# Decode attention with a gated feed-forward: weights in long runs with permuted d and f, loads in another order, down projection by rows

## The chip, the cores and the metric

One core of a Trainium2 chip runs the whole program. The metric is the device time of one execution in microseconds (us). It is about 1.8 to 2 us more than the span that a profile shows, from the first instruction to the last. Repeated executions of the kernel before lie within 0.3 to 0.7 us of each other on one chip, so differences of one microsecond can be read against it. The experiments ran on other chips in three series, each beside the kernel before, whose median was 1316.80, 1316.98 and 1316.93 us there, so medians of different series can be compared.

## The reference, cut to what matters

```python
# B=4 tokens, D=512, H=32 heads of Dh=128, caches of Sk=8192 rows, F=1792, all bf16
x  = A_x
q  = layernorm(x) @ wq                                   # wq 512 x 4096
s  = einsum("bhqd,bhkd->bhqk", q, k_cache) * Dh ** -0.5
o  = einsum("bhqk,bhkd->bhqd", softmax(s), v_cache)
h  = x + o.reshape(B, 1, H * Dh) @ wo                    # wo 4096 x 512
hn = layernorm(h)
h2 = h + (sigmoid(hn @ w_gate) * (hn @ w_up)) @ w_down   # 512 x 1792, 1792 x 512
```

The two caches are 537 MB, the five weights 14 MB. Every byte is read once.

## The kernel before

The caches come in 256 loads of 2 MB, one for each of k and v of each token and head, into a ring of eight slots. One list gives the order of all loads, and the sync engine (SP) issues them in that order, each when its slot is free. v runs ten loads behind k. The v tiles are called v0 to v127 below.

```python
items = [("wq", 0)]
for t in range(NT + LAG):            # NT = 128, LAG = 10
    if t < NT:
        items.append(("k", t))
    if t == NT + 3:
        items.append(("wo", 0))      # ahead of v121
    if t == NT + LAG - 1:
        items.append(("wg", 0))      # ahead of v127
    if t >= LAG:
        items.append(("v", t - LAG))
items += [("wu", 0), ("wd", 0)]      # behind v127
...
# the output weights go where the transposed k was, so their load waits for the last score
op.deps = [sc_of[NT - 1]] if it[0] == "wo" else [consumed[p] for p in prev_of[it]]
```

The weights are loaded so that the contraction index is on the 128 partitions in blocks: `wq`, gate and up with `"(c p) f -> p c f"`, down with `"(t p) f -> p t f"`, the output weights with `"(h p) f -> p h f"`. A matmul has two operands. In the profiles each matmul has two records, a weight load (PEld, 11846 in the kernel before) and the matmul itself (PE, 11846 too), and the weight loads run beside the matmuls (gate and up: 3.06 us of PEld and 3.15 us of PE, both from 1303.79 us). The operand of the weight load is called stationary here, the other one moving. The results are written to PSUM, the accumulators. In the tail of the kernel all weights are the stationary operand, in blocks of 128 adjacent columns, and the activations (4 columns, one a token) are the moving one:

```python
def wo_mms(e, heads, b0, b1, first=False):          # 160 matmuls in all
    ... e.matmul(bH[...], wo_v[:, h, 128 * c:128 * (c + 1)], OT[...], ...)

def pe_gu(e, wv, bk):                               # gate, then up: 56 matmuls each
    for t in range(NFT):                            # NFT = 14
        for c in range(NDC):                        # NDC = 4
            e.matmul(bk[:, B * t:B * t + B], wv[:, c, 128 * t:128 * (t + 1)],
                     hnT[:, B * c:B * c + B], start=(c == 0), stop=(c == NDC - 1))

def pe_down(e):                                     # 56 matmuls, result is h2 transposed
    for c in range(NDC):
        for t in range(NFT):
            e.matmul(bX[:, B * c:B * c + B], wd_v[:, t, 128 * c:128 * (c + 1)],
                     hh_sb[:, B * t:B * t + B], start=(t == 0), stop=(t == NFT - 1))
# then: add h (VectorE), four fp32 transposes, one copy of 4 x 512, output DMA
```

Of the kernel before, what the change touches and what calls it, by code (L numbers as in the profile page):

```python
# [6 lines left out]
FP32 = mybir.dt.float32  # L7
U32 = mybir.dt.uint32
ALU = mybir.AluOpType
ACT = mybir.ActivationFunctionType  # L10
# [3 lines left out]
LAG = 10  # L14
# [58 lines left out]
def bass_sequential_preLN__mha_block_cached__glu_gated_glu__decode_kernel(  # L73
# [12 lines left out]
    B, _sq, D = A_x.shape  # L86
    _, H, S, DH = A_k_cache.shape
    F = B_w_gate.shape[1]
    assert DH == 128 and H == 32 and D == 512 and F % 128 == 0 and B <= 4
    assert S == 8192  # L90
    NDC = D // 128
    NFT = F // 128
    NT = B * H
    NG = NT // GH
    R = S // 128
    TW = R * 128
# [4 lines left out]
    P = prog.add  # L101

    with ExitStack() as es:
        def SB(name, shape, dt):
            return es.enter_context(nc.sbuf_tensor(name, shape, dt))
# [8 lines left out]
        ident = SB("ident", [128, 128], BF16)  # L114
        identf = SB("identf", [128, 128], FP32)
# [5 lines left out]
        xpad = SB("xpad", [128, D], BF16)  # L121
        x_bf = SB("x_bf", [128, D], BF16)
# [16 lines left out]
        hnT = SB("hnT", [128, NDC * B], BF16)  # L139
        sg_sb = SB("sg_sb", [128, NFT * B], FP32)  # L140
        hh_sb = SB("hh_sb", [128, NFT * B], BF16)
        oT_f = SB("oT_f", [128, NDC * B], FP32)
        o_sb = SB("o_sb", [B, D], BF16)

        PS = es.enter_context(nc.psum_tensor("PS", [128, 4096], FP32))
# [2 lines left out]
        bX, bH = bank[6], bank[7]  # L148
# [8 lines left out]
        def ringv(slot):  # L157
            return ring[:, slot, :]


        items = [("wq", 0)]
        for t in range(NT + LAG):
            if t < NT:
                items.append(("k", t))
            if t == NT + 3:
                items.append(("wo", 0))
            if t == NT + LAG - 1:
                items.append(("wg", 0))
            if t >= LAG:
                items.append(("v", t - LAG))  # L170
        items += [("wu", 0), ("wd", 0)]
        slot_of, prev_of, dma_of = {}, {}, {}
        owner = [None] * (NS - 1) + [("qr", 0)]
        uses = [0] * NS
# [21 lines left out]
        def kv_src(t, cache):  # L196
            return cache[t // H, t % H, :, :].rearrange("(p r) d -> p (r d)", p=128)

        dma_x = P("sp", lambda e: e.dma_start(x_bf[0:B, :], A_x.rearrange("b s d -> (b s) d")).then_inc(s_x, 16),
                  sem=s_x, val=16)  # L200

        def load(it):
            kind, t = it
            slot = slot_of.get(it)
            if kind == "wo":
                return [(lambda e: e.dma_start(wo_v, A_wo.rearrange("(h p) f -> p h f", p=128)).then_inc(s_wo, 16),
                         s_wo, 16)]
            if kind == "v" and t == NT - 1:
                ops = []
                for i in range(4):  # L210
                    def f(e, i=i):
                        c0 = i * (TW // 4)
                        return e.dma_start(ringv(slot)[:, c0:c0 + TW // 4],  # L213
                                           kv_src(t, A_v_cache)[:, c0:c0 + TW // 4]).then_inc(s_piece[i], 16)
                    ops.append((f, s_piece[i], 16))
                return ops
            uses[slot] += 1
            sem, val = s_slot[slot], 16 * uses[slot]
            if kind == "k":
                dst, src = ringv(slot), kv_src(t, A_k_cache)  # L220
            elif kind == "v":
                dst, src = ringv(slot), kv_src(t, A_v_cache)
            elif kind == "wq":
                dst, src = wq_v, A_wq.rearrange("(c p) f -> p c f", p=128)
            elif kind == "wg":
                dst, src = wg_v, B_w_gate.rearrange("(c p) f -> p c f", p=128)
            elif kind == "wu":
                dst, src = wu_v, B_w_up.rearrange("(c p) f -> p c f", p=128)
            else:
                dst, src = wd_v, B_w_down.rearrange("(t p) f -> p t f", p=128)  # L230
            return [(lambda e: e.dma_start(dst, src).then_inc(sem, 16), sem, val)]  # L231


# [37 lines left out]
        def pe_xT(e):  # L271
            mm = None
            for c in range(NDC):
                mm = e.matmul(bX[:, B * c:B * c + B], x_bf[0:B, 128 * c:128 * (c + 1)], ident[0:B, 0:B],
                              start=True, stop=True)
            return mm
        p_xT = P("pe", pe_xT, [dma_x, c_ident])

        def pe_xnT(e):
            mm = None  # L280
            for c in range(NDC):
                mm = e.matmul(bH[:, B * c:B * c + B], xpad[:, 128 * c:128 * (c + 1)], ident[:, 0:B],
                              start=True, stop=True)
            return mm
        p_xnT = P("pe", pe_xnT, [d_x, c_ident])
# [20 lines left out]
        for half in range(2):  # L306
            for a in range(4):
                def f(e, half=half, a=a):
                    dst = bass.AP(ring, QR0 + half * 2048 + 32 * a,
                                  [[NS * TW, 128], [256, 8], [128, 2], [1, 32]])  # L310
                    src = bS[half][:, :].rearrange("p (g w e) -> p g e w", g=8, e=2)
                    if half == 0:
                        return e.activation(dst, src, ACT.Copy)
                    return e.tensor_copy(dst, src)  # L314
# [71 lines left out]
        def pe_pv(t, r0=0, r1=R, last=True):  # L386
            it = ("v", t)
            g, hh = t // GH, t % GH
            slot = slot_of[it]
            ob = bO[(g + (1 if t == NT - 1 else 0)) % 2]  # L390

            def f(e):
                mm = None
                for r in range(r0, r1):
                    c0 = (r % 16) * 32 + (r // 16) * 8 + hh
                    mm = e.matmul(ob[:, hh:hh + 1], ringv(slot)[:, r * 128:(r + 1) * 128],  # L396
                                  PT_sb[:, g % 2, c0:c0 + 1], start=(r == 0), stop=(r == R - 1))
                return mm
            deps = [ptc_of[g]]
            if t == NT - 1:  # L400
                deps += [dma_of[it][r0 // 16]]
            else:
                deps += dma_of[it]
            if hh == 0:
                deps.append(oev_of.get(g - 2))
            if t == NT - 1:
                deps.append(oev_of.get(g - 1))
            op = P("pe", f, deps)
            if last:
                pv_of[t] = op  # L410
                consumed[it] = op
# [105 lines left out]
        def wo_mms(e, heads, b0, b1, first=False):  # L517
            mm = None
            for h in heads:
                for c in range(NDC):  # L520
                    mm = e.matmul(bH[:, c * B + b0:c * B + b1], wo_v[:, h, 128 * c:128 * (c + 1)],
                                  OT[:, b0 * H + h:(b1 - 1) * H + h + 1:H],
                                  start=(first and h == heads[0] and c == 0),
                                  stop=(h == H - 1 and c == NDC - 1), skip_group_check=True)
            return mm
# [4 lines left out]
        o_a = oev(gl, 0, GH - 1)  # L530
        P("pe", lambda e: wo_mms(e, range(H - GH, H - 1), B - 1, B), [o_a])
        P("act", lambda e: e.activation(lnst[0:B, 9:10], lnst[0:B, 3:4], ACT.Sqrt), [exp_of[gl]])
        for i in range(4):
            pe_pv(NT - 1, 16 * i, 16 * i + 16, last=(i == 3))
        o_b = oev(gl, GH - 1, GH)
        p_attn = P("pe", lambda e: wo_mms(e, range(H - 1, H), B - 1, B), [o_b])

# [21 lines left out]
                                                  mean_b(20), ALU.mult), [d_rs, d_hc])  # L559
        P("act", lambda e: e.activation(lnst[0:B, 10:11], tst[0:B, 12:13], ACT.Sigmoid), [a_sq])  # L560

        def pe_gu(e, wv, bk):
            mm = None
            for t in range(NFT):
                for c in range(NDC):
                    mm = e.matmul(bk[:, B * t:B * t + B], wv[:, c, 128 * t:128 * (t + 1)],
                                  hnT[:, B * c:B * c + B], start=(c == 0), stop=(c == NDC - 1))
            return mm
        p_g = P("pe", lambda e: pe_gu(e, wg_v, bS[0]), [d_hn, dma_of[("wg", 0)][0]])
# [1 line left out]
        a_sig = P("act", lambda e: e.activation(sg_sb[:, :], bS[0][:, 0:NFT * B], ACT.Sigmoid), [p_g])  # L571
        d_hh = P("dve", lambda e: e.tensor_tensor(hh_sb[:, :], sg_sb[:, :], bS[1][:, 0:NFT * B], ALU.mult), [a_sig, p_u])

        def pe_down(e):
            mm = None
            for c in range(NDC):
                for t in range(NFT):
                    mm = e.matmul(bX[:, B * c:B * c + B], wd_v[:, t, 128 * c:128 * (c + 1)],  # L578
                                  hh_sb[:, B * t:B * t + B], start=(t == 0), stop=(t == NFT - 1))
            return mm  # L580
        p_d = P("pe", pe_down, [d_hh, dma_of[("wd", 0)][0], d_st])
        d_o = P("dve", lambda e: e.tensor_tensor(oT_f[:, :], h2[:, 0, :], bX[:, 0:NB], ALU.add), [p_d])

        def pe_oT(e):
            mm = None
            for c in range(NDC):
                mm = e.transpose(bP[0][0:B, 128 * c:128 * (c + 1)], oT_f[:, B * c:B * c + B], identf[:, :])  # L587
            return mm
        p_oT = P("pe", pe_oT, [d_o, ptc_of[gl], ptc_of[gl - 1]])
        d_out = P("dve", lambda e: e.tensor_copy(o_sb[:, :], bP[0][0:B, 0:D]), [p_oT])  # L590
        consumed[("wg", 0)] = consumed[("wu", 0)] = consumed[("wd", 0)] = p_d

        def sp_out(e):
            e.dma_start(out.rearrange("b s d -> (b s) d"), o_sb[:, :]).then_inc(s_out, 16)
            return e.wait_ge(s_out, 16)
        P("sp", sp_out, [d_out])

        for it in items:
            for op in dma_of[it]:
# [51 lines left out]
```

## Time and profile before

| | before |
|---|---|
| time, median of 4 | 1316.81 us (1316.69 to 1316.97) |
| span of the profiled run | 1314.9 us |
| DMA queue, share of 16 engines | 99.1% |
| landing of the last weights (down) | 1309.44 us |
| from that landing to the end | 5.5 us |

The page of the kernel before says what bounds it. In the second part each digit is the busy share of one fortieth of the span in tenths:

```profile
PE   2453443433343353343344344344334434334425
DMA  9999999999999999999999999999999999999997
GB/s 391 428 427 426 428 426 428 426 426 427 427 427 427 428 427 425 427 427 428 426 427 428 427 426 428 426 428 427 426 427 427 426 428 425 429 426 428 371 381 292
...
q1 hardware_dynamic: 44816, 550.79, 99.1%
```

The DMA engines are busy from end to end at about 427 GB/s and TensorE (PE) is 40% busy. Only in the last three slices does the rate fall. The windows view (start:end, length, busy time and count of PE, PEld, VectorE (DVE), ScalarE (ACT) and GpSimd (POOL), PE clock, DMA share, GB/s) shows a hole there. The clock of 1.00 in these lines is a missing record:

```profile
1200.00:1203.00 3.00, 0.00 (x0) 0.00 (x0) 3.00 (x4) 0.00 (x0) 0.00 (x0) 1.00 0.97 410
1230.00:1233.00 3.00, 0.00 (x0) 0.00 (x0) 3.00 (x4) 0.00 (x0) 0.00 (x0) 1.00 0.71 295
1233.00:1236.00 3.00, 2.29 (x33) 0.90 (x34) 0.99 (x2) 0.00 (x0) 0.00 (x0) 1.00 0.57 246
...
1251.00:1254.00 3.00, 0.00 (x0) 0.00 (x0) 0.00 (x0) 0.00 (x0) 0.00 (x0) 1.00 0.54 190
```

The tail of the kernel before, from the timeline (start us, duration us, engine, line, operation, count, and in brackets the idle time before and what ended it; PEld lines, the weight loads that run beside the matmuls, are left out):

```profile
1290.56 1.87 PE L396 MATMUL PS<-PT_sb,ring 128*128 128x1 bf16 x64 [4.17 <-DMA ring<-in_A_v_cache_dram]
...
1292.29 4.30 PE L521 MATMUL PS<-OT,kT 128*128 128x4 bf16 x156
...
1298.66 1.42 PE L396 MATMUL PS<-PT_sb,ring 128*128 128x1 bf16 x48 [2.07 <-issue]
...
1303.79 3.15 PE L566 MATMUL PS<-hnT,ring 128*128 128x4 bf16 x112 [1.34 <-DVE hnT L557]
...
1309.57 1.64 PE L578 MATMUL PS<-hh_sb,ring 128*128 128x4 bf16 x56 [2.64 <-DMA ring<-in_B_w_down_dram]
1311.24 0.17 DVE L582 TENSOR_TENSOR oT_f<-h,PS 128x16 f32<-128x16 f32 x1 [3.99 <-PE PS L578]
...
1311.47 1.01 PE L587 MATMUL PS<-identf,oT_f 128*4 128x128 f32 x4 [0.27 <-DVE oT_f L582]
1312.52 0.68 DVE L590 CAST o_sb<-PS 4x512 bf16<-4x512 f32 x1 [1.10 <-PE PS L587]
```

Gate and up are 112 matmuls in 3.15 us, 28 ns each. TensorE is then idle for 2.64 us until the down weights land: here the DMA decides, and only the work behind that landing counts.

One more reading is needed. The trace records sixteen completion increments for each load. I read them as one for each of the core's 16 DMA engines; the records do not name the engine. For some loads of the kernel before, worked out from these records:

```
load                  last of 16 at   the sixteen came earlier than that by (us)
an early k            73.54           1.7 ... 1.4, 1.4, 1.4, 1.1, 1.1, 0.7, 0.0, 0.0
a v half way          608.38          8.2 8.1 7.9 7.8 7.5 7.4 7.3 5.1 | 0.4 0.3 0.3 0.3 0.3 0.2 0.1 0.0
v120                  1248.99         17.8 17.6 17.4 17.3 16.9 16.4 16.1 11.8 | 2.3 2.0 1.8 0.6 0.6 0.5 0.3 0.0
output weights        1260.00         10.2 to 9.9 (eight) | 2.2 to 0.0 (eight)
down weights          1309.44         4.7 to 3.7 (eight) | 1.4 to 0.0 (eight)
```

Eight engines come to run ahead of the other eight, by up to 17.8 us just ahead of the output weights; behind them the lead is about 4 us. A load has landed only when the last of the sixteen has come: the matmuls on v120, whose last came at 1248.99 us, begin at 1249.13. So the late eight set the landings.

### The profile page before, as it was taken

The numbers are of one execution on the slowest core, as the hardware profiler recorded it, in microseconds if no ns is written. First come the engines' busy times: TensorE is split into PE (matmuls) and PEld (weight loads), VectorE is DVE, ScalarE is ACT, GpSimd is POOL, SyncE is SP. The second block draws the span as 40 slices with busy tenths as digits, with TensorE's granted clock in tenths as the row PEclk, the third lists the DMA queues.
The fourth block names the chain that finished last, engine by engine and source line by source line (L and its number), as shares of the span: only waits on it lengthen the run. The fifth ranks groups of instructions, "written<-read, shape, count | busy, mean of one in ns | idle before, by whom it ended". The sixth has DMA issues, their size and how long they took to land.

```text
span 1314.9 us, 24889 instructions
## 1 busy us (share of the span) xinstructions
PE 522.6 (40%) x11846; PEld 327.6 (25%) x11846; DVE 629.1 (48%) x640; ACT 38.9 (3%) x86; POOL 9.7 (1%) x17
## 2 busy tenths in 40 slices
PE   2453443433343353343344344344334434334425
PEld 1122222222232232222222222222222223222324
DVE  6975445445444544544544454554544444454300
ACT  3000000000000000000000000000000000000000
POOL 2000000000000000000000000000000000000000
DMA  9999999999999999999999999999999999999997
GB/s 391 428 427 426 428 426 428 426 426 427 427 427 427 428 427 425 427 427 428 426 427 428 427 426 428 426 428 427 426 427 427 426 428 425 429 426 428 371 381 292
DMA packets 44917, 552.37 MB, mean 420 GB/s; under 512 B 4232, under 2 KB 10128, under 8 KB 11664
## 3 DMA queue, kind: packets, MB, share of 16 engines
q1 hardware_dynamic: 44816, 550.79, 99.1%
q8 instruction: 92, 1.51, 0.5%
q14 instruction: 9, 0.07, 0.0%
HBM read 550.77 MB, written 0.00 MB: 419 GB/s over the span
## 4 chain that ended last, share of the span: by engine, by line
DMA 82%; DVE 12%; issue 3%; SPq 2%; PE 1%
DMA ring<-in_A_k_cache_dram 77%; DVE kT L356 11%; DMA ring<-in_A_v_cache_dram 2%; DMA ring<-in_B_w_down_dram 2%; SPq L213 1%; DMA ring<-in_A_wq_dram 1%; DVE Lq L339 0%; SPq L231 0%; PE PS L396 0%; PE PS L373 0%; PE PS L297 0%; DVE ring L314 0%; PE PS L324 0%; PE PS L578 0%; PE PS L587 0%
## 5 line engine op out<-in xcount | busy, mean ns | idle before, releaser
L356 DVE STREAM_TRANSPOSE kT<-ring 128x1024 uint32<-128x1024 uint32 x512 | 592.3, 1213 | 596.0 <-DMA ring<-in_A_k_cache_dram 596.0
L373 PE MATMUL PS<-kT,Lq 128*32 128x512 bf16 x2048 | 242.8, 623 | 663.5 <-DVE kT L356 663.5
L396 PEld LDWEIGHTS PS<-PT_sb,ring 128*128 128x128 bf16 x8192 | 230.1, 104 | 116.1 <-issue 75.5
L396 PE MATMUL PS<-PT_sb,ring 128*128 128x1 bf16 x8192 | 239.3, 165 | 39.7 <-DMA ring<-in_A_v_cache_dram 36.5
L373 PEld LDWEIGHTS PS<-kT,Lq 128*32 128x32 bf16 x2048 | 56.8, 126 | 751.3 <-DVE kT L356 679.8
L435 ACT ACTIVATE negm<-PS 128x1 f32<-128x1 f32 x16 | 2.7, 171 | 1166.9 <-PE PS L431 1166.9
L446 PE MATMUL PS<-LS,onesf 128*128 128x8 f32 x32 | 9.5, 372 | 65.2 <-DVE LS L442 65.2
L468 DVE TENSOR_TENSOR OT<-PS,rinv 128x8 bf16<-128x8 f32 (+2 forms) x17 | 2.0, 115 | 53.4 <-PE PS L396 53.4
L446 PEld LDWEIGHTS PS<-LS,onesf 128*128 128x128 f32 x32 | 8.0, 311 | 66.8 <-DVE LS L442 66.8
L457 PE MATMUL PS<-Sel,E_sb 128*32 128x32 bf16 x1024 | 11.4, 193 | 2.5 <-issue 1.4
L414 DVE TENSOR_REDUCE mx<-PS 128x1 f32<-128x512 f32 x16 | 10.5, 657 | 2.0 <-PE PS L373 2.0
L431 PEld LDWEIGHTS PS<-onesf,rowx 1*128 1x128 f32 x32 | 8.0, 307 | 12.6 <-issue 12.6
L437 ACT ACTIVATE E_sb<-PS,negm 128x512 bf16<-128x512 f32 x16 | 11.0, 687 | 0.7 <-ACT negm L435 0.2
L463 ACT ACTIVATE PT_sb<-PS 128x512 bf16<-128x512 f32 x16 | 9.6, 597 | 27.0 <-PE PS L457 27.0
L457 PEld LDWEIGHTS PS<-Sel,E_sb 128*32 128x32 bf16 x1024 | 9.6, 103 | 2.8 <-issue 1.5
L431 PE MATMUL PS<-onesf,rowx 1*128 1x1 f32 x32 | 9.3, 358 | 0.0
L249 POOL MEMSET Lq<- 128x8208 f32 x1 | 6.9, 6937 | 0.0
L339 DVE CAST Lq<-PS 32x128 bf16<-32x128 f32 x8 | 5.7, 712 | 2.2 <-PE PS L324 2.0
L267 DVE TENSOR_SCALAR xpad<-x_bf,lnst 4x512 bf16<-4x512 bf16 x1 | 6.0, 5993 | 0.0
L420 PE MATMUL PS<-identf,mx 128*1 128x128 f32 x16 | 5.9, 371 | 0.0
L314 DVE CAST ring<-PS 128x512 bf16<-128x512 f32 x4 | 2.5, 684 | 7.2 <-PE PS L297 7.2
L338 ACT ACTIVATE Lq<-PS 32x128 bf16<-32x128 f32 x8 | 5.7, 715 | 4.3 <-PE PS L324 4.1
(69 smaller groups left out, 67.5 us busy)
## 6 DMA issues: line engine op xcount, KB each, us to landing
ring<-in_A_k_cache_dram SPq DMA_DIRECT2D x128, 2048.0 KB, 34.7
ring<-in_A_v_cache_dram SPq DMA_DIRECT2D x127, 2048.0 KB, 35.9
ring<-in_A_wq_dram SPq DMA_DIRECT2D x1, 4096.0 KB, 12.5
kT<-in_A_wo_dram SPq DMA_DIRECT2D x1, 4096.0 KB, 24.3
ring<-in_A_v_cache_dram SPq DMA_DIRECT2D x4, 512.0 KB, 28.0
ring<-in_B_w_gate_dram SPq DMA_DIRECT2D x1, 1792.0 KB, 37.8
ring<-in_B_w_up_dram SPq DMA_DIRECT2D x1, 1792.0 KB, 23.4
ring<-in_B_w_down_dram SPq DMA_DIRECT2D x1, 1792.0 KB, 23.7
```

What stands on the lines that cost most here:

```text
L213: return e.dma_start(ringv(slot)[:, c0:c0 + TW // 4], kv_src(t, A_v_cache)[:, c0:c0 + TW // 4]).then_inc(s_piece[i], 16)
L249: zlq = pool(lambda e: e.memset(Lq[:, :].bitcast(FP32), 0.0))
L267: d_x = P("dve", lambda e: e.tensor_scalar(xpad[0:B, :], x_bf[0:B, :], st[0:B, 0:1], st[0:B, 4:5], op0=ALU.subtract, op1=ALU.mult), [d_r, zx])
L356: return e.transpose(kT[:, buf, i * q:(i + 1) * q].bitcast(U32), ringv(src)[:, i * q:(i + 1) * q].bitcast(U32))
L373: mm = e.matmul(bS[g % 2][32 * j:32 * (j + 1), :], Lq[:, l0:l0 + 32], rhs, start=(hh == 0 and v == 0), stop=(hh == GH - 1 and v == 3), til ...
L396: mm = e.matmul(ob[:, hh:hh + 1], ringv(slot)[:, r * 128:(r + 1) * 128], PT_sb[:, g % 2, c0:c0 + 1], start=(r == 0), stop=(r == R - 1))
L414: mx_of[g] = P("dve", lambda e: e.tensor_reduce(mx[:, :], bS[g % 2][:, :], AX.X, ALU.max), [sc_of[g * GH + GH - 1], p1_of.get(g - 1)])
L431: p2_of[g] = P("pe", lambda e: e.matmul(bX[:, 0:1], rowx[0:1, :], onesf[0:1, 0:1], start=True, stop=True), [d2b_of[g], c_ones])
L437: exp_of[g] = P("act", lambda e: e.activation(E_sb[:, :], bS[g % 2][:, :], ACT.Exp, bias=negm[:, 0:1], scale=SCALE, accum_out=sig[:, 0:1]) ...
L446: L_of[g] = P("pe", lambda e: e.matmul(bX[:, 0:GH], onesf[:, :], LS[:, :], start=True, stop=True), [LS_of[g], a1_of[g], c_ones])
L457: mm = e.matmul(bP[g % 2][32 * a:32 * (a + 1), 32 * rr:32 * rr + 32], E_sb[:, 32 * rr:32 * rr + 32], Sel[:, a, :], start=True, stop=True, ...
L463: ptc_of[g] = P("act", lambda e: e.activation(PT_sb[:, g % 2, :], bP[g % 2][:, :], ACT.Copy), [pt_of[g]] + last_pv)
```

## The change

The intent: long contiguous runs in DRAM for `wq`, gate, up and down, by renumbering d as 4p+c and f as 14p+t; the output weights just ahead of v126 instead of v121, so that the other loads do not queue behind them; all feed-forward weights behind v127; v127 in two pieces instead of four; the input x on the ACT queue; and the down projection by rows, with the activations stationary and the weights moving, so that the result needs no transposes. h is put into the same accumulators ahead of time by small fp32 matmuls against an identity.

```diff
-            if t == NT + 3:
+            if t == NT + LAG - 2:
                 items.append(("wo", 0))
-            if t == NT + LAG - 1:
-                items.append(("wg", 0))
             if t >= LAG:
                 items.append(("v", t - LAG))
-        items += [("wu", 0), ("wd", 0)]
+        items += [("wg", 0), ("wu", 0), ("wd", 0)]
@@ ... x on the ACT queue, v127 in two pieces, down weights in two parts (10 and 4 of t)
-                dst, src = wq_v, A_wq.rearrange("(c p) f -> p c f", p=128)
+                dst, src = wq_v, A_wq.rearrange("(p c) f -> p c f", p=128)
@@ ... gate and up alike; down:
-                dst, src = wd_v, B_w_down.rearrange("(t p) f -> p t f", p=128)
+                          ... B_w_down.rearrange("(p t) f -> p t f", p=128)[:, t0:t1, :]
@@ ... output projection, gate and up: the stationary operand is now strided
-    wo_v[:, h, 128 * c:128 * (c + 1)]
+    wo_v[:, h, c:D:NDC]                    # step 4 elements, 8 bytes
-    wv[:, c, 128 * t:128 * (t + 1)]
+    wv[:, c, t:F:NFT]                      # step 14 elements, 28 bytes
@@ ... h by rows, ahead of gate
+        def pe_h(e):
+            for s_ in range(2):
+                for c in range(NDC):
+                    mm = e.matmul(bP[s_][0:B, c:HD:NDC], h2[:, 0, B * c:B * c + B],
+                                  identf[:, 64 * s_:64 * s_ + 64], start=(c == 0), stop=False, ...)
@@ ... down by rows; the addition, the transposes and the copy of 4 x 512 go
+        for i, (t0, t1) in enumerate(WD_PARTS):
+            for s_ in range(2):
+                    for t in range(t0, t1):
+                        mm = e.matmul(bP[s_][0:B, 0:HD], hh_sb[:, B * t:B * t + B],
+                                      wd_v[:, t, HD * s_:HD * s_ + HD], start=False, ...)
+        o0 = P("act", ... activation(o_sb[:, 0:HD], bP[0][0:B, 0:HD], ACT.Copy) ...)
+        o1 = P("dve", ... tensor_copy(o_sb[:, HD:D], bP[1][0:B, 0:HD]) ...)
```

More of the change, by code (lines that the diff above doesn't have):

```diff
@@ L141, in bass_sequential_preLN__mha_block_cached__glu_gated_glu__decode_kernel @@
         hh_sb = SB("hh_sb", [128, NFT * B], BF16)
-        oT_f = SB("oT_f", [128, NDC * B], FP32)
         o_sb = SB("o_sb", [B, D], BF16)
@@ L158, in ringv @@
             return ring[:, slot, :]
+        WD_PARTS = [(0, 10), (10, NFT)]
         items = [("wq", 0)]
@@ L197, in kv_src @@
             return cache[t // H, t % H, :, :].rearrange("(p r) d -> p (r d)", p=128)
-        dma_x = P("sp", lambda e: e.dma_start(x_bf[0:B, :], A_x.rearrange("b s d -> (b s) d")).then_inc(s_x, 16),
+        dma_x = P("act", lambda e: e.dma_start(x_bf[0:B, :], A_x.rearrange("b s d -> (b s) d")).then_inc(s_x, 16),
                   sem=s_x, val=16)
@@ L209, in load, with f @@
                 ops = []
-                for i in range(4):
+                for i in range(2):
                     def f(e, i=i):
-                        c0 = i * (TW // 4)
-                        return e.dma_start(ringv(slot)[:, c0:c0 + TW // 4],
-                                           kv_src(t, A_v_cache)[:, c0:c0 + TW // 4]).then_inc(s_piece[i], 16)
+                        c0 = i * (TW // 2)
+                        return e.dma_start(ringv(slot)[:, c0:c0 + TW // 2],
+                                           kv_src(t, A_v_cache)[:, c0:c0 + TW // 2]).then_inc(s_piece[i], 16)
                     ops.append((f, s_piece[i], 16))
+                return ops
+            if kind == "wd":
+                ops = []
+                for i, (t0, t1) in enumerate(WD_PARTS):
+                    def f(e, t0=t0, t1=t1, i=i):
+                        return e.dma_start(wd_v[:, t0:t1, :],
+                                           B_w_down.rearrange("(p t) f -> p t f", p=128)[:, t0:t1, :]
+                                           ).then_inc(s_piece[2 + i], 16)
+                    ops.append((f, s_piece[2 + i], 16))
                 return ops
@@ L223, in load @@
             elif kind == "wq":
-                dst, src = wq_v, A_wq.rearrange("(c p) f -> p c f", p=128)
+                dst, src = wq_v, A_wq.rearrange("(p c) f -> p c f", p=128)
             elif kind == "wg":
-                dst, src = wg_v, B_w_gate.rearrange("(c p) f -> p c f", p=128)
-            elif kind == "wu":
-                dst, src = wu_v, B_w_up.rearrange("(c p) f -> p c f", p=128)
+                dst, src = wg_v, B_w_gate.rearrange("(p c) f -> p c f", p=128)
             else:
-                dst, src = wd_v, B_w_down.rearrange("(t p) f -> p t f", p=128)
+                dst, src = wu_v, B_w_up.rearrange("(p c) f -> p c f", p=128)
             return [(lambda e: e.dma_start(dst, src).then_inc(sem, 16), sem, val)]
@@ L273, in pe_xT @@
             for c in range(NDC):
-                mm = e.matmul(bX[:, B * c:B * c + B], x_bf[0:B, 128 * c:128 * (c + 1)], ident[0:B, 0:B],
+                mm = e.matmul(bX[:, B * c:B * c + B], x_bf[0:B, c:D:NDC], ident[0:B, 0:B],
                               start=True, stop=True)
@@ L281, in pe_xnT @@
             for c in range(NDC):
-                mm = e.matmul(bH[:, B * c:B * c + B], xpad[:, 128 * c:128 * (c + 1)], ident[:, 0:B],
+                mm = e.matmul(bH[:, B * c:B * c + B], xpad[:, c:D:NDC], ident[:, 0:B],
                               start=True, stop=True)
@@ L400, in pe_pv @@
             if t == NT - 1:
-                deps += [dma_of[it][r0 // 16]]
+                deps += [dma_of[it][r0 // 32]]
             else:
@@ L520, in wo_mms @@
                 for c in range(NDC):
-                    mm = e.matmul(bH[:, c * B + b0:c * B + b1], wo_v[:, h, 128 * c:128 * (c + 1)],
+                    mm = e.matmul(bH[:, c * B + b0:c * B + b1], wo_v[:, h, c:D:NDC],
                                   OT[:, b0 * H + h:(b1 - 1) * H + h + 1:H],
@@ L532, in bass_sequential_preLN__mha_block_cached__glu_gated_glu__decode_kernel @@
         P("act", lambda e: e.activation(lnst[0:B, 9:10], lnst[0:B, 3:4], ACT.Sqrt), [exp_of[gl]])
-        for i in range(4):
-            pe_pv(NT - 1, 16 * i, 16 * i + 16, last=(i == 3))
+        for i in range(2):
+            pe_pv(NT - 1, 32 * i, 32 * i + 32, last=(i == 1))
         o_b = oev(gl, GH - 1, GH)
@@ L560, in bass_sequential_preLN__mha_block_cached__glu_gated_glu__decode_kernel @@
         P("act", lambda e: e.activation(lnst[0:B, 10:11], tst[0:B, 12:13], ACT.Sigmoid), [a_sq])
+        HD = D // 2
+        def pe_h(e):
+            mm = None
+            for s_ in range(2):
+                for c in range(NDC):
+                    mm = e.matmul(bP[s_][0:B, c:HD:NDC], h2[:, 0, B * c:B * c + B], identf[:, 64 * s_:64 * s_ + 64],
+                                  start=(c == 0), stop=False, skip_group_check=True)
+            return mm
+        P("pe", pe_h, [d_h, c_identf, ptc_of[gl], ptc_of[gl - 1]])
         def pe_gu(e, wv, bk):
@@ L565, in pe_gu @@
                 for c in range(NDC):
-                    mm = e.matmul(bk[:, B * t:B * t + B], wv[:, c, 128 * t:128 * (t + 1)],
+                    mm = e.matmul(bk[:, B * t:B * t + B], wv[:, c, t:F:NFT],
                                   hnT[:, B * c:B * c + B], start=(c == 0), stop=(c == NDC - 1))
@@ L572, in bass_sequential_preLN__mha_block_cached__glu_gated_glu__decode_kernel, with pe_down @@
         d_hh = P("dve", lambda e: e.tensor_tensor(hh_sb[:, :], sg_sb[:, :], bS[1][:, 0:NFT * B], ALU.mult), [a_sig, p_u])
-        def pe_down(e):
-            mm = None
-            for c in range(NDC):
-                for t in range(NFT):
-                    mm = e.matmul(bX[:, B * c:B * c + B], wd_v[:, t, 128 * c:128 * (c + 1)],
-                                  hh_sb[:, B * t:B * t + B], start=(t == 0), stop=(t == NFT - 1))
-            return mm
-        p_d = P("pe", pe_down, [d_hh, dma_of[("wd", 0)][0], d_st])
-        d_o = P("dve", lambda e: e.tensor_tensor(oT_f[:, :], h2[:, 0, :], bX[:, 0:NB], ALU.add), [p_d])
-        def pe_oT(e):
-            mm = None
-            for c in range(NDC):
-                mm = e.transpose(bP[0][0:B, 128 * c:128 * (c + 1)], oT_f[:, B * c:B * c + B], identf[:, :])
-            return mm
-        p_oT = P("pe", pe_oT, [d_o, ptc_of[gl], ptc_of[gl - 1]])
-        d_out = P("dve", lambda e: e.tensor_copy(o_sb[:, :], bP[0][0:B, 0:D]), [p_oT])
-        consumed[("wg", 0)] = consumed[("wu", 0)] = consumed[("wd", 0)] = p_d
+        p_d = []
+        for i, (t0, t1) in enumerate(WD_PARTS):
+            for s_ in range(2):
+                def pe_down(e, t0=t0, t1=t1, s_=s_):
+                    mm = None
+                    for t in range(t0, t1):
+                        mm = e.matmul(bP[s_][0:B, 0:HD], hh_sb[:, B * t:B * t + B], wd_v[:, t, HD * s_:HD * s_ + HD],
+                                      start=False, stop=(t == NFT - 1), skip_group_check=True)
+                    return mm
+                p_d.append(P("pe", pe_down, [d_hh, dma_of[("wd", 0)][i]]))
+        o0 = P("act", lambda e: e.activation(o_sb[:, 0:HD], bP[0][0:B, 0:HD], ACT.Copy), [p_d[2]])
+        o1 = P("dve", lambda e: e.tensor_copy(o_sb[:, HD:D], bP[1][0:B, 0:HD]), [p_d[3]])
+        consumed[("wg", 0)] = consumed[("wu", 0)] = consumed[("wd", 0)] = p_d[3]
         def sp_out(e):
@@ L595, in sp_out @@
             return e.wait_ge(s_out, 16)
-        P("sp", sp_out, [d_out])
+        P("sp", sp_out, [o0, o1])
         for it in items:
```

## The prediction

> **What bounds the kernel now.** DMA: the slices show the DMA engines 9/10 busy throughout, 427 GB/s in the middle; the DMA queue took 99.1% of 16 engines' span; the chain of waits is 82% DMA. From 2.3 to 1309.4 us some engine always transfers; then a tail of 5.5 us (timeline): down projection 1.64, addition 0.17, transposes 1.0, copy 0.68, output DMA about 1.7.
>
> The windows show the DMA share falling to 0.57 at 1233-1236 us and 0.54 at 1251-1254: the sync queue stood 21.4 us waiting for the last score before the output-weight load, then 18.3 us issuing the next value load behind that load's 4096 small packets. The lost share sums to about 7.8 us, which I do not count as gain. The sixteen completion increments of each load show eight engines up to 17 us ahead of the other eight by then. Landings are set by the late eight, which never starve: v120 lands at 1248.99, the output weights 11.0 us later, then a value load each 4.9 us. The hole eats only the early engines' lead; moving the load moves the hole.
>
> **What changes, on the late engines.**
> - Start: the x load leaves the sync queue; weights start 0.4 us earlier.
> - Packet records: 16 KB takes 615 ns, 4 KB about 168, 3.5 KB 143, 1 KB 41 to 50. [...] The last value goes from 5.36 us to an estimated 4.95, gate and up from 4.32 and 4.62 to about 4.3 each, down from 4.63 to about 4.4: together about 1 us. The output weights keep 1 KB rows.
> - The last landing comes at about 1308.0.
> - Tail: after the last part only 8 matmuls of 256 columns (estimate 0.9 us), two half copies side by side (0.4), output DMA (1.7): 3.2 us if nothing before is late. Eight fp32 matmuls (about 1.3 us) put h into PSUM under the layer norm.
>
> **The risk is TensorE before the end.** Feed-forward weights now follow the last value, so from v126's landing (about 1290.1) TensorE must do 64 value matmuls, 156 of the output projection (4.3 us), the last value, layer norm, gate, up, then 20 down matmuls. At today's weight-load rate (27 ns each) these end just as the last weights land. But the permutation makes weight loads strided: 8 bytes for output weights, 28 for gate and up. [...] Unslowed, I get a span of 1311.3; gate and up at half speed (3.1 us each), 1313.5; output weights slow too, about 1318.
>
> **Prediction.** The time is 2 us over the span: 1314.6 us, range 1312.4 to 1318.5. Chances: over 2% faster 0.01, within 2% 0.98, over 2% slower 0.01.
>
> **Shown by:** landings (last weights about 1308, each value 4.9 us on the late half); the DMA-share hole still there, about 30 us later; spacing of weight loads in gate and up; the wait ahead of the last 8 down matmuls (DMA or TensorE's own work); tail from last landing to end 3 to 6 us.
>
> **What would make it wrong:** strided weight loads at four times the time (slower than before); late engines gaining when the early ones keep streaming (2 to 8 us faster); fp32 matmuls delaying gate.

Two sentences, one on small packets and one on strided weight loads, are cut from the recorded text where it is marked: they did not come from the traces of this case. The sum itself came to this: last landing at 1308.0 us and a tail of 3.2 us, a span of 1311.3 with nothing slowed; 1313.5 if gate and up take twice their 3.1 us together; the point, 1314.6 less the 2 us, is a span of 1312.6, between the two. That a strided weight load might go at half speed was my supposition; no trace had shown what a step costs. The estimates for the loads follow from packet times: 256 packets of 8 KB, 309 ns each in the trace of the kernel before (the query weights, median), on 16 engines are 4.94 us for the last value. Averaged, the packets of that trace took 616 ns at 16 KB, 170 at 4 KB, 143 at 3.5 KB and 46 to 50 at 1 KB. Two estimates do not say from what they are: 0.9 us for the last 8 matmuls (the kernel after: 109 ns each, 0.87 us, at the full clock, and 213 ns each at the half clock) and 1.3 us for the fp32 matmuls (1.87 us there).

## The result, and the profile after

| | before | after |
|---|---|---|
| time, median of 4 | 1316.81 us | 1319.51 us (1318.65 to 1320.16) |
| ratio | | 1.002, 95% interval 1.0003 to 1.0037 |
| span of the profiled run | 1314.9 us | 1316.9 us |
| landing of the query weights | 13.71 us | 12.90 us |
| landing of the last weights | 1309.44 us | 1308.13 us |
| from there to the end | 5.5 us | 8.8 us |

Ratios are the mean time of one kernel's fast runs over that of the other's of the same rounds, so they are not quite the ratios of the medians. Their intervals reach about 0.15% (2 us) to each side; for differences of a few microseconds I also give the single runs. In a second series of five rounds the changed kernel took 1320.09 us against 1316.93, ratio 1.0025 (1.0011 to 1.0039). By the rule of 2% this is "same", but it is slower, and it was predicted faster.

The slices of the page after, with a line for the clock that TensorE was granted:

```profile
PEclk7555555555555555555555555555555555555555
GB/s 400 429 426 428 427 427 427 427 428 425 426 428 426 428 427 426 426 427 428 427 428 426 427 426 428 428 427 428 425 427 427 427 426 427 427 427 427 427 319 266
```

The rate now holds until the last two slices. The windows of the kernel after show that the hole has moved, and the last three of them what the clock does at the end (0.50 in this view is half of TensorE's full clock):

```profile
1230.00:1233.00 3.00, 0.00 (x0) 0.00 (x0) 3.00 (x4) 0.00 (x0) 0.00 (x0) 0.50 1.02 426
...
1269.00:1272.00 3.00, 0.90 (x34) 0.81 (x31) 0.00 (x0) 0.00 (x0) 0.00 (x0) 0.50 0.54 224
1272.00:1275.00 3.00, 1.87 (x64) 1.79 (x64) 0.00 (x0) 0.00 (x0) 0.00 (x0) 0.50 0.53 188
...
1308.00:1311.00 3.00, 2.62 (x34) 2.20 (x34) 0.21 (x1) 0.00 (x0) 0.00 (x0) 0.50 0.00 0
1311.00:1314.00 3.00, 3.00 (x21) 2.00 (x20) 0.00 (x0) 0.00 (x0) 0.00 (x0) 0.68 0.00 0
1314.00:1317.00 3.00, 0.67 (x7) 0.30 (x4) 0.41 (x1) 0.37 (x1) 0.00 (x0) 1.00 0.00 1
```

The timeline of the tail after:

```profile
1289.82 1.87 PE L402 MATMUL PS<-PT_sb,ring 128*128 128x1 bf16 x64 [15.06 <-DMA ring<-in_A_v_cache_dram]
...
1291.55 5.34 PE L527 MATMUL PS<-OT,kT 128*128 128x4 bf16 x156
...
1297.61 1.84 PE L402 MATMUL PS<-PT_sb,ring 128*128 128x1 bf16 x64 [0.71 <-issue]
...
1301.04 1.87 PE L575 MATMUL PS<-identf,h 128*4 128x64 f32 x16
...
1302.84 6.88 PE L583 MATMUL PS<-hnT,ring 128*128 128x4 bf16 x112
...
1310.10 4.57 PE L597 MATMUL PS<-ring,hh_sb 128*4 128x256 bf16 x28 [0.38 <-DVE hh_sb L589]
1314.27 0.37 ACT L601 ACTIVATE o_sb<-PS 4x256 bf16<-4x256 f32 x1 [7.65 <-PE PS L597]
1314.71 0.41 DVE L602 CAST o_sb<-PS 4x256 bf16<-4x256 f32 x1 [4.67 <-PE PS L597]
```

From 1289.8 us on TensorE waits for no load any more. The last weights land at 1308.13 us, before the down projection has even begun (1310.10 us). Gate and up take 6.88 us instead of 3.15, 60 ns a matmul. The 28 matmuls of the down projection take 4.57 us. The chain that ended last says the same; for the kernel after its end reads (start, duration, what):

```profile
1289.82 1.87 PE PS L402 x64
1291.69 5.20 PE PS L527 x156
1296.89 0.71 issue
...
1301.11 1.80 PE PS L575 x16
1302.91 6.83 PE PS L583 x112
...
1310.10 4.59 PE PS L597 x28
```

Before, the corresponding stretch of the chain was one DMA entry for the down weights:

```profile
1285.71 23.72 DMA ring<-in_B_w_down_dram
```

The change has taken the end of the kernel from the DMA and given it to TensorE.

Inside the down projection the starts of successive matmuls, taken from the trace, are 213 ns apart up to the fourteenth (167 ns between the first two) and 109 ns apart for the last fourteen; the trace's clock record goes from 0.5 to 1.0 at 1312.90 us, in between.

### The profile page after: what moved, and what is told of

It is laid out like the page before. It is cut to its first block, busy times and chain, and to the rows that moved or that the text cites. A ratio compares the mean times of both kernels' runs of the same rounds, so it can differ in the third digit from the quotient of the medians.

```text
span 1316.9 us, 24857 instructions
## 1 busy us (share of the span) xinstructions
PE 530.5 (40%) x11830; PEld 334.7 (25%) x11830; DVE 628.1 (48%) x639; ACT 39.3 (3%) x87; POOL 9.7 (1%) x17
## 4 chain that ended last, share of the span: by engine, by line
DMA 83%; DVE 12%; issue 3%; PE 2%; DVEq 0%
DMA ring<-in_A_k_cache_dram 77%; DVE kT L362 11%; DMA ring<-in_A_v_cache_dram 5%; DMA ring<-in_A_wq_dram 1%; PE PS L583 1%; DVE Lq L345 0%; PE PS L527 0%; PE PS L597 0%; PE PS L402 0%; PE PS L303 0%; DVE ring L320 0%; PE PS L330 0%; PE PS L575 0%; DVE mx L420 0%; PE PS L548 0%
## 5 line engine op out<-in xcount | busy, mean ns | idle before, releaser
L583 PE MATMUL PS<-hnT,ring 128*128 128x4 bf16 x112 | 6.9, 199 | 0.0
L583 PEld LDWEIGHTS PS<-hnT,ring 128*128 128x128 bf16 x112 | 6.8, 158 | 0.2 <-issue 0.2
```

Source lines behind the costliest of these rows:

```text
L583: mm = e.matmul(bk[:, B * t:B * t + B], wv[:, c, t:F:NFT], hnT[:, B * c:B * c + B], start=(c == 0), stop=(c == NDC - 1))
```

## The experiments

My theory after the result: the DMA side did what was predicted, and the loss is TensorE's, in two terms, the strided weight loads of gate and up and the row-wise down projection at half the clock. Rivals: the order of the loads costs (or should have gained) time by itself, or one of the two terms is hidden.

### The order of the output weights alone (e1_wo_only)

The kernel before with one line changed:

```diff
-            if t == NT + 3:
+            if t == NT + LAG - 2:
                 items.append(("wo", 0))
```

> The kernel before with one part of the change alone: the output-weight load is placed ahead of v126 instead of ahead of v121. My theory (landings are set by the eight late DMA engines, which never starve, so the hole in the DMA share eats only the early engines' lead): the hole is still there, about 30 us later and of the same size, the last weights land at 1309.4 to 1310.5 us, the span is 1314.5 to 1316. Rival (the hole is lost DMA time that better order gives back, 7.8 us by the lost share): last landing 1302 to 1306, span 1307 to 1311.

Measured: 1317.17 us, ratio 1.0003 (0.9988 to 1.0018); the last weights land at 1310.12 us, the profiled span is 1315.6 us. The windows of this kernel:

```profile
1230.00:1233.00 3.00, 0.00 (x0) 0.00 (x0) 3.00 (x4) 0.00 (x0) 0.00 (x0) 1.00 1.01 421
...
1269.00:1272.00 3.00, 1.45 (x55) 1.37 (x52) 0.00 (x0) 0.00 (x0) 0.00 (x0) 1.00 0.58 243
1272.00:1275.00 3.00, 1.57 (x58) 1.57 (x59) 0.00 (x0) 0.00 (x0) 0.00 (x0) 1.00 0.52 187
```

The hole has moved and is as deep (summed as missing GB/s against 427: 7.8 us before, 8.1 here), and the time has not changed. Across the hole the lead of the early eight engines falls from 17.8 to 4.3 us (before: 17.8 to 3.9), while the landings keep their pace: the lost DMA share was the early engines standing still, which nobody waits for. So neither the gain nor the loss is in the place of this load.

### f not permuted (e2_f_plain)

```diff
-    wv[:, c, t:F:NFT]
+    wv[:, c, 128 * t:128 * (t + 1)]
-    B_w_down.rearrange("(p t) f -> p t f", p=128)[:, t0:t1, :]
+    B_w_down.rearrange("(t p) f -> p t f", p=128)[:, t0:t1, :]
```

> The changed kernel with the permutation of f undone alone: gate and up take 128 adjacent columns again and the down weights come in 1 KB rows. Theory (28-byte strided weight loads made gate and up cost 60 ns a matmul instead of 27, and that lies on the path to the end): gate and up fall from 6.9 to about 3.1 us, down stays at 0.213 us a matmul at the half clock, the span falls from 1316.9 by 1.6 to 3.4 us, to 1313.5 to 1315.3. Rival (the time is in the down projection alone, gate and up are hidden behind the landing of the last weights): span within 0.5 us of 1316.9.

Measured: 1316.50 us, 3.0 us below the changed kernel's 1319.51; ratio to before 0.9999 (0.9982 to 1.0016). Its four runs took 1316.10 to 1317.19 us, those of the changed kernel 1318.65 to 1320.16. The timeline of its tail:

```profile
1303.09 3.15 PE L583 MATMUL PS<-hnT,ring 128*128 128x4 bf16 x112
...
1307.60 4.49 PE L597 MATMUL PS<-ring,hh_sb 128*4 128x256 bf16 x28 [1.36 <-DMA ring<-in_B_w_down_dram]
```

Gate and up are back at 28 ns a matmul, and the down projection has to wait for its weights again. The stride cost 3.7 us of TensorE time and 3.0 us of the end, because the wait takes some of it back. The down projection itself is as slow as before this undoing, and from the last landing (1308.81 us) to the end this kernel still takes 5.5 us.

### Down projection by columns (e3_down_cols) and both undone (e5_plain_cols)

The first keeps the permutation of f and puts the old orientation back, in the two parts of the new loads; the second does this and leaves f plain.

```diff
-    mm = e.matmul(bP[s_][0:B, 0:HD], hh_sb[:, B * t:B * t + B], wd_v[:, t, HD * s_:HD * s_ + HD], ...)
+    mm = e.matmul(bX[:, B * c:B * c + B], wd_v[:, t, c:D:NDC], hh_sb[:, B * t:B * t + B], ...)
@@ ... pe_h goes; the addition, four transposes and one copy of 4 x 512 come back
```

> The changed kernel with the down projection by rows undone alone: weights are the stationary operand again (56 matmuls of 4 columns, weight loads at a stride of 8 bytes), the addition, four fp32 transposes and one whole copy follow, the early fp32 matmuls for h are gone. Theory (28 matmuls of 256 columns at half the TensorE clock cost 4.6 us where I had counted 3.1): down takes about 1.9 us, transposes, addition and copy give back 1.5 us, span 1315.3 to 1316.3, so 0.6 to 1.6 us below the changed kernel, and no dependence on the clock. Rival (rows are right and only the strided gate and up cost): span 1316.9 or more.

> Both undone: f plain and down in columns, everything else of the change kept (d permuted, order of loads, last value in two, x on the ACT queue). Theory: TensorE waits for the last down weights again, tail from last landing to end 4.3 to 5 us, span 1312.8 to 1313.8, about 1.5 us below the kernel before, which is the DMA side of the change alone. If the order of the loads itself costs time, the span is 1315 or more.

Measured: e3_down_cols 1317.57 us, ratio to before 1.0006 (0.9992 to 1.0021), 1.9 us below the changed kernel. Its profiled run was the slowest of its four, with a span of 1316.7 us, above the range I gave, because v126 landed 0.8 us later in that run; the other three spans are 1315.4 to 1315.8. Its runs (1317.14 to 1318.53 us) only just do not overlap with those of the changed kernel. Measured: e5_plain_cols 1314.77 us, ratio 0.9985 (0.997 to 1.0), 4.7 us below the changed kernel; its span of 1313.6 us and its 4.5 us from the last landing to the end are as expected. The timeline of e3_down_cols:

```profile
1303.77 6.88 PE L574 MATMUL PS<-hnT,ring 128*128 128x4 bf16 x112 [1.34 <-DVE hnT L564]
...
1311.04 2.02 PE L588 MATMUL PS<-hh_sb,ring 128*128 128x4 bf16 x56 [0.38 <-DVE hh_sb L580]
```

and of e5_plain_cols:

```profile
1303.50 3.14 PE L574 MATMUL PS<-hnT,ring 128*128 128x4 bf16 x112 [1.33 <-DVE hnT L564]
...
1307.87 2.00 PE L588 MATMUL PS<-hh_sb,ring 128*128 128x4 bf16 x56 [1.23 <-DMA ring<-in_B_w_down_dram]
```

The two terms add up, to within the half microsecond by which two medians of the changed kernel itself differ (1319.51 and 1320.09 us): 3.0 and 1.9 us alone, 4.7 together. The second is the whole row-wise form, with the fp32 matmuls for h: in the kernel after, gate starts 0.46 us after its input hnT is ready (1302.38 us), because they are still running; without them, in e5_plain_cols, 0.06 us. Without both terms the rest of the change is a gain of 2.0 us on the kernel before (all four runs lie below all of the kernel before, though the interval just reaches 1.0). It is not the loads alone, as I had expected: in the profiled run, the slowest of the four, the last landing is 0.4 us earlier (1309.07 us) and the tail behind it 1.0 us shorter, because only the second part of the down matmuls waits for it. The rows looked cheap because 28 matmuls replace 56 and the transposes go, but 56 matmuls of 4 columns cost 2.0 us and 28 of 256 columns 4.5.

### What a step costs (e4_stride)

```diff
+    for sd in (1, 2, 3, 4, 7, 8, 14):          # ahead of v126's matmuls, where TensorE is idle
+        ... 48 times: e.matmul(bS[1][:, 0:4], Lq[:, 32:32 + 128 * sd:sd], PT_sb[:, 0, 0:4], start=True, stop=True)
```

> The changed kernel with a measurement put into TensorE's 15 us of idle time ahead of v126: seven groups of 48 weight loads of 128 columns with matmuls of 4 columns, taken from a constant tile at column steps of 1, 2, 3, 4, 7, 8 and 14 elements of 2 bytes; their results are thrown away. Theory[...]: 27 ns at steps 1 to 4, or 34 at 4 as the output projection shows, and about 60 ns at 8 and 14 alike, with 7 between. Rival (the time grows with the step): 8 clearly below 14. The span stays within 1 us of the changed kernel's.

The rule that the theory was named after is cut from this text; it came from no trace.

Measured, as the distance from one matmul to the next in the trace, stalls left out:

```
step (elements)     1      2      3        4        7        8     14
step (bytes)        2      4      6        8        14       16    28
ns a matmul        27     27    26-30    33-34    53-54     60    60
```

Of the steps measured, 16 and 28 bytes cost the same 60 ns, so the rival falls. Why the cost grows as it does up to there was not shown. A permutation in which neighbours are two elements apart costs no more than adjacent columns (27 ns), one of 14 as much as any step measured (60 ns). All this is one run, at a recorded clock of 0.5. One expectation was missed: the span was 1323.1 us instead of about 1317. The added block did not fit into the idle time, because TensorE stood still for 2.0 us twice within it:

```profile
1274.70 2.62 PE L521 MATMUL PS<-PT_sb,Lq 128*128 128x4 bf16 x93
...
1279.34 4.75 PE L521 MATMUL PS<-PT_sb,Lq 128*128 128x4 bf16 x128 [2.02 <-issue]
...
1286.11 6.95 PE L521 MATMUL PS<-PT_sb,Lq 128*128 128x4 bf16 x115 [2.01 <-issue]
```

"issue" means that nothing in the profile was waited for. Exactly 128 matmuls lie between the two stalls, with their weight loads 256 instructions, and each stall ends 1.3 to 1.4 us after a packet of 16,384 bytes of the queue that the page calls "instruction" has ended (at 1278.00 and 1284.70 us). The same pattern is in the kernels before and after ahead of v127's matmuls (the 2.07 and 0.71 us above; packets ended at 1297.36 and 1296.40, and the matmuls began at 1298.66 and 1297.61). What TensorE stood still for was not shown: these times are all that the traces give, and no experiment took a cause away.

### d not permuted (e9_d_plain), beside the changed kernel again

```diff
-    wo_v[:, h, c:D:NDC]
+    wo_v[:, h, 128 * c:128 * (c + 1)]
@@ ... x, wq, gate and up rows in blocks of 128 again; f stays permuted, down stays by rows
```

> The changed kernel with the permutation of d undone alone (x, output weights, gate and up rows in their old order; f stays permuted). Theory: the output projection's weight loads are adjacent again, its 156 matmuls fall from 5.3 to 4.3 us, and as TensorE's own work sets the end from v126 on, the span falls by 0.7 to 1.3 us against the changed kernel; gate and up stay at 6.9 us; the feed-forward weights land up to 1.5 us later in their shorter rows and nobody waits for them. Rival (the length of the weight rows sets the end): the span rises by the later landing.

> The changed kernel as it is, again, on the chip and in the rounds of the next one. Theory: runs fall on two levels, about 1318.7 us where the clock is released to full within the down projection (mean granted clock recorded as 0.509) and about 1 us more where it is not (all 28 matmuls then cost 0.213 us; recorded as 0.508, or 1.0 where the records are missing).

Measured in the same five rounds: the changed kernel 1320.09 us, e9_d_plain 1319.87 us (ratio to before 1.0022, 1.0009 to 1.0034). My expectation of 0.7 to 1.3 us was wrong. The timelines show why; first e9_d_plain, then the changed kernel in this series:

```profile
1291.92 4.30 PE L527 MATMUL PS<-OT,kT 128*128 128x4 bf16 x156
...
1298.30 1.85 PE L402 MATMUL PS<-PT_sb,ring 128*128 128x1 bf16 x64 [2.08 <-issue]
```

```profile
1291.79 5.34 PE L527 MATMUL PS<-OT,kT 128*128 128x4 bf16 x156
...
1297.82 1.85 PE L402 MATMUL PS<-PT_sb,ring 128*128 128x1 bf16 x64 [0.69 <-issue]
```

The output projection did fall from 5.34 to 4.30 us, but the stall behind it grew from 0.69 to 2.08 us, which took the microsecond back. At the same recorded clock the runs do not differ either: with 0.509 one run of the changed kernel took 1319.24 us and four of e9_d_plain 1319.30 to 1319.87. The step of 8 bytes is therefore not part of the loss in this kernel, though it looks like one in the durations. The rival falls too: the last landing came 0.5 us later (1308.35 against 1307.83 us) and nobody waited for it.

The times of the changed kernel have two levels. In the first series the two runs with a mean clock of 0.509 took 1318.65 and 1319.05 us, the two that are marked 1.0, which I take for missing clock records, 1319.98 and 1320.16. In this series its one run with a mean clock of 0.509 took 1319.24 us; the other four, marked 1.0, 1320.06 to 1320.30. The profiled one among these runs is the 0.509 run, so a trace of the slower level is missing, and that its 28 matmuls all ran at 213 ns is an inference. The sums fit it: in the first series 14 matmuls ran at the full clock, and at 104 ns more each 1318.65 us would become 1320.1; in this series the release came later, 11 ran at the full clock, and 1319.24 us would become 1320.4. One run of e2_f_plain is recorded at 0.508, which I read as without the release, and it is the slowest of its four (1317.19 us against 1316.10 and 1316.33 at 0.509).

### A version that beats both (e6_groups, e7_pairs)

From the above: keep gate and up at adjacent or nearly adjacent columns; keep rows for down, but put the four quarters of d into four column groups of the array, as the score matmuls are, which run four at a time (16 of 512 columns in 1.90 us, a round every 0.43 us, in the trace of the kernel before); and give TensorE its output projection earlier.

```diff
-            if t == NT + LAG - 2:
+            if t == NT + LAG - 3:               # output weights ahead of v125
@@ ... most of the output projection between v125's and v126's matmuls; pe_h behind up
+    for t in range(t0, t1):
+        for j in range(4):
+            mm = e.matmul(bP[0][32 * j:32 * j + B, 0:128], hh_sb[:, B * t:B * t + B],
+                          wd_v[:, t, 128 * j:128 * (j + 1)], ..., tile_position=(0, 32 * j), ...)
@@ ... four copies of 4 x 128, two on ACT, two on VectorE
@@ e6_groups: f plain.   e7_pairs: f in pairs
+    wv[:, c, 256 * (t // 2) + t % 2:256 * (t // 2) + t % 2 + 255:2]
+    B_w_down.rearrange("(s p k) f -> p s (k f)", p=128, k=2)[:, t0 // 2:t1 // 2, :]
```

> A version built from what the experiments say: the changed kernel with f plain, the output-weight load one value earlier (ahead of v125) and most of the output projection between v125 and v126, h put into PSUM after up instead of ahead of gate, and the down projection by rows but with the four quarters of d in four column groups of the array that run at the same time (56 matmuls of 128 columns, four at a time at 0.107 us). Theory: TensorE is then ahead of the DMA everywhere and only what follows the last landing counts: last landing 1308.3 to 1309.3, then about 0.6 us of matmuls, 0.5 of copies, 1.7 of output DMA, span 1311.2 to 1312.6, 4 to 5.5 us below the changed kernel. If the four groups do not overlap, 1.3 us more.

> The same, with f permuted in pairs: weight loads at a step of 2 elements (4 bytes) and down weights in runs of 2 KB. Theory: gate and up stay at 27 to 30 ns a matmul and the down weights land 0.3 us earlier: span 0.2 to 0.5 us below the version with f plain. If a step of 2 elements already slows weight loads, gate and up show it, but the span hardly moves, since TensorE waits there.

Measured: e6_groups 1313.99 us, ratio 0.9978 (0.9963 to 0.9993); e7_pairs 1313.40 us, ratio 0.9973 (0.9957 to 0.999). Both profiled spans are 1311.6 us, last landings 1308.41 and 1308.21. Several things change at once here; what each of them gives was not measured, nor was the 0.6 us between the two medians explained. The timeline of e7_pairs:

```profile
1300.86 1.66 PE L574 MATMUL PS<-hnT,ring 128*128 128x4 bf16 x56 [1.34 <-DVE hnT L564]
...
1303.80 1.65 PE L574 MATMUL PS<-hnT,ring 128*128 128x4 bf16 x56 [1.29 <-DMA ring<-in_B_w_up_dram]
...
1307.07 2.10 PE L598 MATMUL PS<-ring,hh_sb 128*4 128x128 bf16 x56 [0.52 <-DMA ring<-in_B_w_down_dram]
...
1309.21 0.60 DVE L607 CAST o_sb<-PS 4x128 bf16<-4x128 f32 x2 [3.44 <-PE PS L598]
```

Gate and up at a step of 4 bytes are as fast as at adjacent columns (1.66 and 1.65 us in e6_groups), and up waits for its weights again; the down matmuls go four in 0.107 us (in the trace of e6_groups) at the half clock. After the last landing 3.4 us remain.

### An attempt on the late engines (e8_eight)

```diff
+            if kind == "v" and t in (100, 112):
+                ... 16 transfers of 8 partitions each instead of one of 128
```

> The version with f plain and column groups, with two value loads (v100, v112) cut into 16 transfers of 8 partitions each[...]. It tests that the end is set by the eight late engines alone. [...] If neither half sets the end (rival), the span stays within 1.5 us of the version without.

A clause and two sentences are cut from this text: they rested on which engines the cut loads would use, which no trace here shows. The two cases were a span of 1302 to 1305 us and one of 1320 to 1323 us.

Measured: span 1355.5 us, one run, correct. None of the three expectations holds. While the cut loads were under way, packets of 16 KB took 0.9 to 1.2 us on average instead of 0.615, and the landings behind them came 22.0 us later than in e6_groups after the first cut load and 44.1 us after the second. Which engines the cut loads ran on no run here shows, since the packets do not name their engine. Something slowed the packets that I did not foresee, and it hides what the experiment was to show, so which eight engines are late, and why, stays open.

## Why the prediction was wrong

- **Right: what bounded the kernel before, and the hole.** The hole moved by about 30 us and was worth nothing (e1_wo_only).
- **Right: the last landing.** Predicted about 1308.0 us, measured 1308.13; v126 predicted 1290.1, measured 1289.78.
- **Right as a risk, too small in the number: strided gate and up.** I put the point of the prediction between "unslowed" (3.1 us) and "half speed" (6.2). Measured: 6.88 us. Undoing f alone gives 3.0 us back.
- **Wrong: "Tail: after the last part only 8 matmuls of 256 columns (estimate 0.9 us)", and with it the 20 in front of them.** This is the step that failed: the cost of a row-wise matmul. The estimate is 0.11 us each, and the prediction does not say from what. It is what 256 columns cost at the full clock, as the last 14 show (109 ns each, clock record 1.0); but TensorE was at the half clock when the down projection began (record 0.5), and there one took 213 ns. The trace of the kernel before already had that pace: its score matmuls, 16 of 512 columns in 1.90 us, sit in four column groups and run four at a time, a round every 0.43 us, so 256 columns would take 0.21. Dividing 1.90 by 16, as if they ran one after the other, gives 0.12 us and hides this.

  Here the clock record went to 1.0 2.8 us after these matmuls began, when half of them were done, and 2.6 to 4.8 us after in the four other traces that have them and a clock record; through the 6.88 us of gate and up just before, with 4 columns each, it had stayed at 0.5. What brings the release was not shown.

  Measured for the 28: 4.57 us against the estimate's 3.1. e2_f_plain shows this step without the strided gate and up: 5.5 us from the last landing to the end, where the prediction had 3.2. Undoing the row-wise form gives 1.9 us back. That is less than the 2.55 us by which the matmuls alone get shorter, because addition, transposes and the whole copy return.
- **Wrong: "these end just as the last weights land".** TensorE began its down projection 2.0 us after the last landing, because of gate and up; the cost of the rows came on top, and the tail from landing to end became 8.8 us, not 3 to 6. Even with gate and up at 27 ns a matmul (e2_f_plain) the first 20 down matmuls were not done until more than 2 us after that landing.
- **Named as a risk, not in the sum: "fp32 matmuls delaying gate".** They took 1.87 us instead of 1.3 and delayed gate by about 0.4.
- **Not the cause, though it looked like one:** the output projection's 5.34 us in place of 4.30 (e9_d_plain).
- **The range** had too little above: my own case "output weights slow too, about 1318" was a span, and with 2 us added it lay outside the 1318.5 us that I gave.

## What to carry to other kernels

A layout that lengthens DMA runs may stride the stationary operand: look at the step in bytes before the run length, since here runs of 4 to 14 KB instead of 1 to 3.5 KB brought the last landing forward by about 1 us (undoing f moved it back by 0.7, undoing d by 0.5), and a step of 28 bytes cost 3. When the DMA decides, ask of a hole in its busy share whether the engine that finishes last stands still in it: here the early ones did (their lead fell from 17.8 to 4.3 us), and moving the hole was worth nothing (ratio 1.0003 in e1_wo_only); look at the sixteen completion times of the single loads. And cost a matmul in a short burst at the clock that the trace shows for that stretch (here half: 213 ns for 256 columns, against 109 at the full clock), from a matmul of the same form in the trace, after asking whether those in the trace ran side by side.

## What the runs of this case measured of the hardware

- Strided weight loads (e4_stride, one run, recorded clock 0.5): with a weight load of 128 bf16 columns, one matmul of 4 columns came every 27 ns at steps of 2 and 4 bytes, 33 to 34 at 8, 53 to 54 at 14, 60 at 16 and 28 bytes.
- Stalls that wait for nothing in the profile, in bursts of short matmuls: 0.7 to 2.1 us, 128 matmuls with their weight loads apart in e4_stride, ending 1.2 to 1.4 us after an instruction packet of 16,384 bytes (e4_stride, and the kernels before and after). One of them took back the gain of e9_d_plain.
- Loads cut into blocks of 8 adjacent partitions (e8_eight, one run): two loads of 2 MB delayed all that followed by about 22 us each. What slowed the packets was not shown.
- The sixteen completions of a load drift apart into two groups of eight: by 17.8 us over 1249 us of even loads in the kernel before.
- Clock records can be missing altogether. The kept trace of the kernel before has none and is marked 1.0, yet its score matmuls keep the half-clock pace (16 of them in 1.90 us, a round of 512 columns every 0.43 us; the same in the kernel after, where the record says 0.5), and runs of this kernel marked 1.0 and 0.508 take the same time (1316.88 and 1316.71 us).
